# Six wide block products instead of five in the second MLP product of a transformer block on one Trainium2 core

## The chip, the cores and the metric

The kernel runs on one core of one Trainium2 chip. A core has a matrix engine (TensorE, PE in the profile, PEld for its weight loads), a vector engine (VectorE, DVE), a scalar engine (ScalarE, ACT), GpSimd (POOL) and SyncE (SP), which issues most transfers. They work side by side, each through its own queue in order, and wait for each other through semaphores. Matmul results go to eight banks of PSUM (512 float32 values a partition each); VectorE and ScalarE read them from there. The metric is the time of one execution on the device in microseconds.

## What is computed

A block with two parts over x of shape (1, 2048, 512), float32: linear attention with a softmax feature map, and a token-mixing MLP. The change lies in the last product of the second part.

```python
h = x + attention(layernorm(x))
u = gelu(einsum("bsd,sf->bdf", layernorm(h), w1) + b1)   # (B, D, F), F = 1792
y = einsum("bdf,fs->bds", u, w2) + b2                    # (B, D, S), S = 2048
out = h + transpose(y, 0, 2, 1)                          # (B, S, D)
```

## The kernel before, in words

**Split numbers.** Matmuls run on float32 operands cut into a high part and a low part (`whi` and `wlo` for weights, the two halves of an operand `un` or `uf` for the activations). A product of two such numbers takes three terms: high by high, high by low, low by high.

**Tiles and steps of the second product.** S is cut into 16 token tiles of 128, taken in 8 token pairs `sp`; F into 14 tiles, taken in 7 feature pairs `p`; D into two halves of 256. A step is one (sp, p), 56 in all, in the order of `STEPS`: the seven feature pairs of the first token pair, then of the second, and so on. A step is a 2x2 by 2x2 block product, done with seven block multiplications in place of eight; each multiplies one of seven sums of weight blocks (index a) with one of seven sums of activation blocks (index b) and adds into a bank. The table `PROD` names for each multiplication a, b, the bank and, where it is given, the half of the bank.

**Wide and narrow.** A multiplication is done in one of two forms. `wide` (L1106) sends the high weight against both parts of the activations in one matmul of 512 columns, whose two products stand in the two halves of the bank, and the low weight against the high part in one of 256 columns, added into the first half. The halves are summed later. `narrow` (L1110) takes three matmuls of 256 columns that all add into one half; two multiplications that belong to different sums so share a bank. Before, five multiplications of a step are wide and two are narrow; a token pair needs six banks. The last token pair uses another table, `LAST`, in which all seven are narrow, in four banks.

**Order on TensorE.** The order of TensorE, VectorE and ScalarE is written out by hand (`manual_schedule`). The first step of a token pair (p = 0, the opening step) is one multiplication after another (`products`). The steps p = 1 to 4 go by groups of up to two in `steps`: first all 512-column matmuls of both, then for each the 256-column ones and the narrow products. The steps p = 5 and 6 (the closing block) go through `products` together: each multiplication for both steps, so that the banks are finished one after another. Banks are dealt in turn over all eight (`n_bank`), from three pools.

**Evictions.** After the closing block, ScalarE copies one half of bank 0 (`e`, L1162) and the second halves of the last three banks (`low`, L1164), and VectorE adds up the rest in nine operations (L1165 to L1169 and four of L1172) into `ot`. GpSimd adds `ot` and `low` to the output in memory by accumulating transfers.

**Weights.** w2 comes in groups of two steps: SyncE loads `wraw` (L973), VectorE forms the seven sums (L857 to L859, called by `sums_w2`), ScalarE rounds them to `whi` (L992, `hi_w2`), VectorE takes the difference as `wlo` (L1002, `lo_w2`). There are two buffers for `wlo` and three for `whi`, so each waits until TensorE is done with an older group. These calls stand at every second step. In even token pairs (0, 2, 4, 6) one such call falls into the closing block, and `lo_w2` and `hi_w2` stand between the first two and the last two of the L1172 operations, with the sums behind them; in odd pairs the last call falls at p = 5, so `lo_w2` and the sums stand ahead of the evictions.

Of the kernel before, what the change touches and what calls it, by code (L numbers as in the profile page):

```python
# [11 lines left out]
AF = mybir.ActivationFunctionType  # L12
ALU = mybir.AluOpType
# [6 lines left out]
NT = S // P  # L20
KD = D // P
NF = F // P
NP = NF // 2
HD = D // 2
GRP = 2
# [13 lines left out]
def block_kernel(ctx: ExitStack, tc: tile.TileContext, x, xT, wT, phic, wo, w1, b1, w2, b2,  # L39
                 kvmask, ident_in, out):  # L40
    nc = tc.nc
# [487 lines left out]
    def keep(shape, dt, name, i):  # L529
        return keep_pool.tile(shape, dt, name=name, tag=f"keep{i}")  # L530
# [325 lines left out]
    def sums_of(raw):  # L856
        nc.vector.tensor_add(raw[:, 0:2], raw[:, 1].unsqueeze(1).to_broadcast([P, 2, raw.shape[2]]), raw[:, 2:4])  # L857
        nc.vector.tensor_add(raw[:, 5], raw[:, 1], raw[:, 2])
        nc.vector.tensor_add(raw[:, 6], raw[:, 4], raw[:, 5])  # L859
# [106 lines left out]
    def load_w2(g):  # L966
        slot = g % 3 if g < 4 else (3, 1, 2, 0)[g % 4]
        shape = [P, 7, GRP * P]
        if slot == 3:
            RAW[g] = raw3 if g == 4 else hp.tile(shape, F32, name="wraw3", bufs=1)  # L970
        else:
            RAW[g] = hold(shape, F32, "wraw", slot)
        nc.sync.dma_start(RAW[g][:, 1:5], w2[g])  # L973

    def sums_w2():

        g = done["sums"]
        if g == NGR:
            return
        done["sums"] += 1  # L980
        if g not in RAW:
            load_w2(g)
        sums_of(RAW[g])

    def hi_w2():

        g = done["hi"]
        if g == NGR:
            return
        done["hi"] += 1  # L990
        WH[g] = keep([P, 7, GRP * P], F32R, "whi", g % 3)
        nc.scalar.activation(WH[g], RAW[g], AF.Copy)  # L992

    def lo_w2():

        g = done["lo"]
        if g == NGR:
            return
        done["lo"] += 1
        shape = [P, 7, GRP * P]  # L1000
        wl_ = hp.tile(shape, F32R, name="wlo1", bufs=1) if g % 2 else keep(shape, F32R, "wlo", 3)
        nc.vector.tensor_sub(wl_, RAW[g], WH[g])  # L1002
        for i, step in enumerate(STEPS[g * GRP:(g + 1) * GRP]):
            AW[step] = WH[g][:, :, i * P:(i + 1) * P], wl_[:, :, i * P:(i + 1) * P]
# [80 lines left out]
    for p in range(NEAR, NP):  # L1085
# [1 line left out]
    wst.close()  # L1087
    uo = ctx.enter_context(tc.tile_pool(name="uo", bufs=2, reuse_waits="tile"))

    PROD = ((2, 1, 0, None), (5, 5, 1, None), (0, 0, 2, 0), (1, 4, 2, 1), (3, 6, 3, None), (6, 2, 4, None),  # L1090
            (4, 3, 5, None))

    def products(sp, ps, order):
        for a, b, bk, half in order:
            if half is None:
                for low in range(2):
                    for p in ps:
                        wide(sp, p, a, b, bk, low)
            else:
                for p in ps:  # L1100
                    narrow(sp, p, a, b, bk, half)

    def wide(sp, p, a, b, bk, low):
        w, u = AW[sp, p][low][:, a], UB[p, b]
        o, u = (bank[bk][:, 0], u[:, 0]) if low else (bank[bk], u)
        nc.tensor.matmul(o, w, u, start=p == 0 and not low, stop=p == NP - 1, skip_group_check=True)  # L1106

    def narrow(sp, p, a, b, bk, half):
        for i, (x, y) in enumerate(((0, 0), (0, 1), (1, 0))):
            nc.tensor.matmul(bank[bk][:, half], AW[sp, p][x][:, a], UB[p, b][:, y], start=p == 0 and half == 0 and i == 0,  # L1110
                             stop=p == NP - 1 and i == 2, skip_group_check=True)

    def steps(sp, ps, order):
        for p in ps:
            for a, b, bk, half in order:
                if half is None:
                    wide(sp, p, a, b, bk, 0)
        for p in ps:
            for a, b, bk, half in order:
                if half is None:  # L1120
                    wide(sp, p, a, b, bk, 1)
            for a, b, bk, half in order:
                if half is not None:
                    narrow(sp, p, a, b, bk, half)

    def flat(a):
        return a.rearrange("p k d -> p (k d)")
# [3 lines left out]
    for n, (sp, p) in enumerate(STEPS):  # L1131
        t = 2 * sp
        last = t + 2 == NT
        if n % GRP == 0 and p < NP - 1:
            lo_w2()
            hi_w2()
            sums_w2()
        if p == 0:
            bank = []
            for _ in range(6):  # L1140
                pool = (ps_f, ps_q, ps_b, ps_b)[n_bank % 8 // 2]
                bank.append(pool.tile([P, 2, HD], F32, name="py", tag="pu"))
                n_bank += 1
        order = LAST if last else PROD
        run_on = 3 if last else 2
        if p == 0:
            products(sp, [p], order)
            continue
        if p < NP - run_on:
            if n % GRP == 0 or p == 1:  # L1150
                steps(sp, range(p, min(p + GRP - n % GRP, NP - run_on)), order)
            continue
        if p < NP - 1:
            continue
        products(sp, range(NP - run_on, NP), order)
        e = uo.tile([P, 2, HD], F32, name="e")
        u2 = uo.tile([P, HD], F32, name="u2", bufs=1)
        u3 = uo.tile([P, HD], F32, name="u3")
        if not last:
            ot = uo.tile([P, 2, 2, HD], F32, name="ot", bufs=1)  # L1160
            low = uo.tile([P, 3, HD], F32, name="low")
            nc.scalar.activation(e[:, 1], bank[0][:, 0], AF.Copy)  # L1162
            for i in range(3):
                nc.scalar.activation(low[:, i], bank[3 + i][:, 1], AF.Copy)  # L1164
            nc.vector.tensor_add(e[:, 1], bank[0][:, 1], e[:, 1])  # L1165
            nc.vector.tensor_sub(u2, bank[1][:, 0], e[:, 1])
            nc.vector.tensor_add(u2, bank[1][:, 1], u2)
            nc.vector.tensor_sub(u3, u2, bank[2][:, 0])
            nc.vector.scalar_tensor_tensor(e[:, 0], bank[2][:, 1], -1.0, u2, op0=ALU.mult, op1=ALU.subtract)  # L1169

            def out_block(i, h, o, add):
                nc.vector.scalar_tensor_tensor(ot[:, i, h], o, b2s[:, t + i:t + i + 1], add, op0=ALU.add, op1=ALU.add)  # L1172

            out_block(0, 0, bank[2][:, 1], u3)
            out_block(0, 1, bank[3][:, 0], u3)
            nc.gpsimd.dma_start(out[t * P:(t + 1) * P, :], flat(ot[:, 0]), accum_op=ALU.add)  # L1176
            if n % GRP == 0:
                lo_w2()
                hi_w2()
            out_block(1, 0, bank[4][:, 0], e[:, 0])  # L1180
            out_block(1, 1, bank[5][:, 0], e[:, 1])
            nc.gpsimd.dma_start(out[(t + 1) * P:(t + 2) * P, :], flat(ot[:, 1]), accum_op=ALU.add)
            nc.gpsimd.dma_start(out[t * P:(t + 1) * P, HD:D], low[:, 0], accum_op=ALU.add)
            nc.gpsimd.dma_start(out[(t + 1) * P:(t + 2) * P, :], flat(low[:, 1:3]), accum_op=ALU.add)
            if n % GRP == 0:
                sums_w2()
            continue

        hb = [uo.tile([P, 2, HD], F32, name=f"hb{i}", bufs=1) for i in range(2)]
        for i in range(2):  # L1190
            nc.sync.dma_start(flat(hb[i]), out[(t + i) * P:(t + i + 1) * P, :])
            nc.vector.tensor_scalar(hb[i], hb[i], b2s[:, t + i:t + i + 1], None, op0=ALU.add)
        nc.scalar.activation(e[:, 1], bank[0][:, 0], AF.Copy)
        nc.vector.tensor_add(hb[1][:, 1], bank[0][:, 0], hb[1][:, 1])
        nc.vector.tensor_sub(u2, bank[0][:, 1], e[:, 1])
        nc.vector.tensor_sub(hb[1][:, 0], hb[1][:, 0], u2)
        nc.vector.tensor_sub(u3, u2, bank[1][:, 0])
        nc.vector.tensor_add(hb[0], hb[0], u3.unsqueeze(1).to_broadcast([P, 2, HD]))
        nc.vector.tensor_add(hb[0][:, 0], bank[1][:, 1], hb[0][:, 0])
        nc.vector.tensor_sub(hb[1][:, 0], hb[1][:, 0], bank[1][:, 1])  # L1200
        nc.vector.tensor_add(hb[0][:, 1], bank[2][:, 0], hb[0][:, 1])
        nc.sync.dma_start(out[t * P:(t + 1) * P, :], flat(hb[0]))
        for k, o, q in ((0, bank[2][:, 1], nc.scalar), (1, bank[3][:, 0], nc.sync)):
            nc.vector.tensor_add(hb[1][:, k], o, hb[1][:, k])
            q.dma_start(out[(t + 1) * P:NT * P, k * HD:(k + 1) * HD], hb[1][:, k])
# [49 lines left out]
```

## Time and profile before

| | |
|---|---|
| median of 3 runs | 518.52 us (518.47 to 518.72) |
| the profiled execution, its own time | 518.56 us |
| its span, first to last instruction | 516.8 us |
| granted TensorE clock | 1.00 |
| first row of the second product (`py`), and the last (start) | 354.0 us, 513.3 us |
| length of a token pair from the second to the seventh | 17.24 and 17.26 us in turn |

A row of the timeline gives the start, the duration and, for several instructions in one row, their count; the engine, the line, the operation, its output and inputs and the shape. In brackets stands how long the engine was idle before it and what released it. A row of busy time by stretch gives, for each engine, the busy time and the number of instructions that started there, then TensorE's granted clock, the DMA share and the rate. Durations of matmuls overlap, so their cost is read from the distance of their starts.

### The profile page before, as it was taken

To read this page: it belongs to the slowest core of one execution; us is meant where nothing else is said; L and a number is where in the kernel's file an instruction comes from. 1 tells how busy PE (TensorE), PEld (TensorE's weight loads), DVE (VectorE), ACT (ScalarE), POOL (GpSimd) and SP (SyncE) were. 2 spreads that over 40 slices of the span, in tenths; PEclk is the share of its full clock that TensorE was granted. 3 is DMA by queue.
4 is the path that set the end of the run, shared out by engine and by line. 5 is a ranking of instruction groups with operands and counts; after the bars stand their busy time and mean duration, and the time that the engine had idled before them with its cause. 6 is when DMAs were issued, how large, how long until landed. Compare 5 with 4: busy or idle time off the path is not lost.

```text
span 516.8 us, 9476 instructions
## 1 busy us (share of the span) xinstructions
PE 510.9 (99%) x3595; PEld 442.9 (86%) x3595; DVE 445.5 (86%) x789; ACT 296.8 (57%) x494; POOL 245.0 (47%) x188
## 2 busy tenths in 40 slices
PE   9999999999999999999999999999999999999997
PEld 8888888887877778777788899998889999899997
DVE  6893999986799998777796998989989898988985
ACT  6998944434255876668976643457653434434430
POOL 2479799975999999985343200000002212212220
PEclk9999999999999999999999999999999999999999
DMA  8744310000041324334322233374135787677843
GB/s 313 270 127 122 81 53 29 1 1 3 12 154 41 103 84 140 124 124 122 115 89 83 82 105 104 99 245 141 43 123 117 162 192 171 119 162 159 191 50 77
DMA packets 36300, 58.56 MB, mean 113 GB/s; under 512 B 3744, under 2 KB 19360, under 8 KB 36256
## 3 DMA queue, kind: packets, MB, share of 16 engines
q1 hardware_dynamic: 31648, 50.85, 31.3%
q0 software_dynamic: 4032, 6.42, 9.9%
q8 instruction: 28, 0.46, 0.4%
q10 hardware_dynamic: 576, 0.69, 0.4%
q14 instruction: 16, 0.13, 0.1%
HBM read 46.81 MB, written 11.14 MB: 112 GB/s over the span
## 4 chain that ended last, share of the span: by engine, by line
PE 89%; POOL 7%; DVE 2%; ACT 1%; issue 1%; POOLq 0%
PE py L1106 17%; PE pu L936 12%; PE py L1110 10%; PE pu L66 7%; PE pu L67 7%; PE pu L68 7%; PE pv L67 3%; PE pv L68 3%; PE pv L66 3%; PE pk_ps L66 2%; PE pk_ps L68 2%; PE pk_ps L67 2%; POOL ez L456 2%; POOL eq L474 2%; PE po L68 2%; PE tn L548 2%
## 5 line engine op out<-in xcount | busy, mean ns | idle before, releaser
L1176 POOL DMA_DIRECT2D out<-ot x7 | 6.2, 884 | 142.1 <-DVE ot L1172 142.1
L992 ACT ACTIVATE whi<-wraw 128x1792 fp32r<-128x1792 f32 x28 | 47.6, 1701 | 44.1 <-DVE wraw L859 20.3
L1002 DVE TENSOR_TENSOR wlo<-wraw,whi 128x1792 fp32r<-128x1792 f32 x28 | 56.6, 2021 | 8.4 <-PE py L1110 6.9
L67 PE MATMUL pu<-hs,whi 128*128 128x512 f32 x128 | 50.3, 393 | 1.2 <-POOL hs L62 1.2
L66 PE MATMUL pu<-hs,whi 128*128 128x512 f32 x128 | 50.1, 399 | 0.0
L1106 PE MATMUL py<-uf,whi 128*128 128x512 f32 x175 | 48.4, 393 | 0.0
L68 PE MATMUL pu<-hs,wlo 128*128 128x512 f32 x128 | 48.0, 390 | 0.0
L897 ACT ACTIVATE whi<-wraw 128x896 fp32r<-128x896 f32 x24 | 22.9, 954 | 31.2 <-PE pu L936 26.4
L456 POOL TENSOR_TENSOR ez<-eq,zB 128x1024 f32<-128x1024 f32 x16 | 38.3, 2399 | 4.4 <-ACT zB L503 4.4
L1110 PE MATMUL py<-uf,whi 128*128 128x256 f32 x210 | 39.0, 283 | 0.0
L936 PE MATMUL pu<-ht,whi 128*128 128x256 f32 x192 | 35.6, 283 | 0.0
L208 POOL TENSOR_TENSOR pk<-pk,sk 128x1024 f32<-128x1024 f32 x16 | 30.9, 1938 | 7.3 <-DVE sk L207 7.2
L62 POOL TENSOR_TENSOR hs<-hb,hs 128x512 fp32r<-128x512 f32 x16 | 22.4, 1400 | 23.9 <-ACT hs L61 23.8
L550 ACT ACTIVATE pht<-tn 128x512 f32<-128x512 f32 x32 | 17.4, 595 | 28.4 <-PE tn L548 28.3
L474 POOL TENSOR_TENSOR eq<-eq,w 128x1024 f32<-128x1024 f32 x16 | 32.4, 2028 | 1.3 <-DVE w L471 1.2
L1110 PEld LDWEIGHTS py<-uf,whi 128*128 128x128 f32 x210 | 32.7, 192 | 0.0
L1106 PEld LDWEIGHTS py<-uf,whi 128*128 128x128 f32 x175 | 29.8, 189 | 3.5
L212 POOL TENSOR_TENSOR zacc<-zacc,pk 128x1024 f32<-128x1024 f32 x13 | 31.2, 2399 | 0.5
L1106 PEld LDWEIGHTS py<-uf,wlo 128*128 128x128 f32 x175 | 27.9, 190 | 4.0
L66 PEld LDWEIGHTS pu<-hs,whi 128*128 128x128 f32 x128 | 24.1, 188 | 7.2 <-issue 2.5
L936 PEld LDWEIGHTS pu<-ht,whi 128*128 128x128 f32 x192 | 30.0, 192 | 0.0
L1110 PE MATMUL py<-uf,wlo 128*128 128x256 f32 x105 | 29.7, 283 | 0.0
(207 smaller groups left out, 1625.0 us busy)
## 6 DMA issues: line engine op xcount, KB each, us to landing
wraw<-in_w SPq DMA_DIRECT2D x28, 512.0 KB, 4.5
wraw<-in_w SPq DMA_DIRECT2D x48, 256.0 KB, 2.8
xraw<-in_xT SPq DMA_DIRECT2D x16, 256.0 KB, 3.1
xh<-in_x SPq DMA_DIRECT2D x16, 256.0 KB, 2.7
h<-in_x SPq DMA_DIRECT2D x16, 256.0 KB, 2.7
out<-h SPq DMA_DIRECT2D x14, 256.0 KB, 2.7
out<-ot POOLq DMA_DIRECT2D x14, 256.0 KB, 4.8
wraw<-in_wT SPq DMA_DIRECT2D x12, 256.0 KB, 4.6
```

The lines of the kernel that those rows point to most:

```text
L66: nc.tensor.matmul(o, ah, bh, start=first, stop=False)
L67: nc.tensor.matmul(o, ah, bl, start=False, stop=False)
L68: nc.tensor.matmul(o, al, bh, start=False, stop=last)
L208: nc.gpsimd.tensor_mul(heads(PK[t]), heads(PK[t]), sk.unsqueeze(2).to_broadcast([P, 2 * H, DH]))
L212: nc.gpsimd.tensor_add(zacc, zacc, PK[t])
L456: nc.gpsimd.tensor_mul(EZ[t], EQ[t], zB)
L474: nc.gpsimd.tensor_mul(heads(EQ[t]), heads(EQ[t]), W[t].rearrange("p g c h -> p (g c h)").unsqueeze(2).to_broadcast([P, 2 * H, DH]))
L936: nc.tensor.matmul(ACC[p][bk][:, half], WS[p, i][x][:, a], hb[b][y], start=i == 0 and half == 0 and k == 0, stop=i == NT // 2 - 1 and k == ...
L992: nc.scalar.activation(WH[g], RAW[g], AF.Copy)
L1002: nc.vector.tensor_sub(wl_, RAW[g], WH[g])
L1106: nc.tensor.matmul(o, w, u, start=p == 0 and not low, stop=p == NP - 1, skip_group_check=True)
L1110: nc.tensor.matmul(bank[bk][:, half], AW[sp, p][x][:, a], UB[p, b][:, y], start=p == 0 and half == 0 and i == 0, stop=p == NP - 1 and i == ...
```

## The change

The multiplication (0, 0), which was narrow in half 0 of bank 2, becomes wide in bank 2; (1, 4) stays narrow and moves to half 0 of a bank of its own; the rest move up by one. A token pair has seven banks, the last pair four (it was dealt six and used four). VectorE gets one more subtraction, of the second half of bank 2. The two `lo_w2`/`hi_w2` calls move behind the last eviction, but not in the pair before the last (`ahead`); in odd pairs the sums that stood at p = 5 move behind the evictions. In the first token pair the seventh multiplication is held back to the second step, and done there for both.

```diff
-    PROD = ((2, 1, 0, None), (5, 5, 1, None), (0, 0, 2, 0), (1, 4, 2, 1), (3, 6, 3, None), (6, 2, 4, None),
-            (4, 3, 5, None))
+    PROD = ((2, 1, 0, None), (5, 5, 1, None), (0, 0, 2, None), (1, 4, 3, 0), (3, 6, 4, None), (6, 2, 5, None),
+            (4, 3, 6, None))
...
         if n % GRP == 0 and p < NP - 1:
             lo_w2()
             hi_w2()
-            sums_w2()
+            if p < NP - 2 or last:
+                sums_w2()
         if p == 0:
             bank = []
-            for _ in range(6):
+            for _ in range(4 if last else 7):
...
         if p == 0:
-            products(sp, [p], order)
+            products(sp, [p], order[:-1] if n == 0 else order)
+            continue
+        if n == 1:
+            steps(sp, [p], order[:-1])
+            products(sp, [0, p], order[-1:])
             continue
...
-                nc.scalar.activation(low[:, i], bank[3 + i][:, 1], AF.Copy)
+                nc.scalar.activation(low[:, i], bank[4 + i][:, 1], AF.Copy)
...
             nc.vector.tensor_sub(u3, u2, bank[2][:, 0])
-            nc.vector.scalar_tensor_tensor(e[:, 0], bank[2][:, 1], -1.0, u2, op0=ALU.mult, op1=ALU.subtract)
+            nc.vector.tensor_sub(u3, u3, bank[2][:, 1])
+            nc.vector.scalar_tensor_tensor(e[:, 0], bank[3][:, 0], -1.0, u2, op0=ALU.mult, op1=ALU.subtract)
...
-            if n % GRP == 0:
+            ahead = t + 4 == NT
+            if ahead:
                 lo_w2()
                 hi_w2()
-            out_block(1, 0, bank[4][:, 0], e[:, 0])
-            out_block(1, 1, bank[5][:, 0], e[:, 1])
+            out_block(1, 0, bank[5][:, 0], e[:, 0])
+            out_block(1, 1, bank[6][:, 0], e[:, 1])
+            if n % GRP == 0 and not ahead:
+                lo_w2()
+                hi_w2()
...
-            if n % GRP == 0:
-                sums_w2()
+            sums_w2()
```

TensorE in the closing block of the first token pair, third and fourth multiplication, for both steps (`py` and its number is a bank, `uf` an operand of the activations). Before:

```order
L1110 MATMUL py_4488<-uf_4433,whi_4479 128x256 x2
L1110 MATMUL py_4488<-uf_4433,wlo_4524 128x256
L1110 MATMUL py_4488<-uf_4459,whi_4526 128x256 x2
L1110 MATMUL py_4488<-uf_4459,wlo1_4564 128x256
L1110 MATMUL py_4488<-uf_4446,whi_4479 128x256 x2
L1110 MATMUL py_4488<-uf_4446,wlo_4524 128x256
L1110 MATMUL py_4488<-uf_4465,whi_4526 128x256 x2
L1110 MATMUL py_4488<-uf_4465,wlo1_4564 128x256
```

and now:

```order
L1106 MATMUL py_4488<-uf_4433,whi_4479 128x512
L1106 MATMUL py_4488<-uf_4459,whi_4525 128x512
L1106 MATMUL py_4488<-uf_4433,wlo_4523 128x256
L1106 MATMUL py_4488<-uf_4459,wlo1_4561 128x256
L1110 MATMUL py_4489<-uf_4446,whi_4479 128x256 x2
L1110 MATMUL py_4489<-uf_4446,wlo_4523 128x256
L1110 MATMUL py_4489<-uf_4465,whi_4525 128x256 x2
L1110 MATMUL py_4489<-uf_4465,wlo1_4561 128x256
```

Twelve matmuls became ten, and they fill two banks instead of one.

TensorE in the opening step of the second token pair, from its second multiplication on (in brackets what a row waits for). Before:

```order
L1106 MATMUL py_4653<-un0_3275,whi_4526 128x512
L1106 MATMUL py_4653<-un0_3275,wlo1_4564 128x256
L1110 MATMUL py_4654<-un0_3275,whi_4526 128x256 [waits DVE_49]
L1110 MATMUL py_4654<-un0_3275,whi_4526 128x256
L1110 MATMUL py_4654<-un0_3275,wlo1_4564 128x256
L1110 MATMUL py_4654<-un0_3275,whi_4526 128x256 x2
L1110 MATMUL py_4654<-un0_3275,wlo1_4564 128x256
L1106 MATMUL py_4655<-un0_3275,whi_4526 128x512 [waits DVE_49,PE_49]
L1106 MATMUL py_4655<-un0_3275,wlo1_4564 128x256
L1106 MATMUL py_4656<-un0_3275,whi_4526 128x512 [waits DVE_49]
```

and now:

```order
L1106 MATMUL py_4648<-un0_3275,whi_4525 128x512 [waits DVE_49]
L1106 MATMUL py_4648<-un0_3275,wlo1_4561 128x256
L1106 MATMUL py_4649<-un0_3275,whi_4525 128x512 [waits DVE_49,PE_49]
L1106 MATMUL py_4649<-un0_3275,wlo1_4561 128x256
L1110 MATMUL py_4650<-un0_3275,whi_4525 128x256 [waits DVE_49,PE_49]
L1110 MATMUL py_4650<-un0_3275,whi_4525 128x256
L1110 MATMUL py_4650<-un0_3275,wlo1_4561 128x256
L1106 MATMUL py_4651<-un0_3275,whi_4525 128x512 [waits DVE_49]
L1106 MATMUL py_4651<-un0_3275,wlo1_4561 128x256
L1106 MATMUL py_4652<-un0_3275,whi_4525 128x512 [waits DVE_49]
```

The second bank already waits for VectorE, where the third did; two multiplications wait for two semaphores, where one did.

VectorE at the end of the second token pair, an odd one. Before:

```order
L857 TENSOR_TENSOR wraw_4760<-wraw_4760 128x512
L858 TENSOR_TENSOR wraw_4760<-wraw_4760 128x256
L859 TENSOR_TENSOR wraw_4760<-wraw_4760 128x256
L1165 TENSOR_TENSOR e_4797<-py_4652,e_4797 128x256
L1166 TENSOR_TENSOR u2_4798<-py_4653,e_4797 128x256
L1167 TENSOR_TENSOR u2_4798<-py_4653,u2_4798 128x256
L1168 TENSOR_TENSOR u3_4799<-u2_4798,py_4654 128x256
L1169 SCALAR_TENSOR_TENSOR e_4797<-py_4654,u2_4798 128x256
L1172 SCALAR_TENSOR_TENSOR ot_4800<-py_4654,b2s_65,u3_4799 128x256
L1172 SCALAR_TENSOR_TENSOR ot_4800<-py_4655,b2s_65,u3_4799 128x256
L1172 SCALAR_TENSOR_TENSOR ot_4800<-py_4656,b2s_65,e_4797 128x256
L1172 SCALAR_TENSOR_TENSOR ot_4800<-py_4657,b2s_65,e_4797 128x256
```

and now:

```order
L1002 TENSOR_TENSOR wlo1_4747<-wraw_4673,whi_4710 128x1792
L1170 TENSOR_TENSOR e_4781<-py_4647,e_4781 128x256
L1171 TENSOR_TENSOR u2_4782<-py_4648,e_4781 128x256
L1172 TENSOR_TENSOR u2_4782<-py_4648,u2_4782 128x256
L1173 TENSOR_TENSOR u3_4783<-u2_4782,py_4649 128x256
L1174 TENSOR_TENSOR u3_4783<-u3_4783,py_4649 128x256
L1175 SCALAR_TENSOR_TENSOR e_4781<-py_4650,u2_4782 128x256
L1178 SCALAR_TENSOR_TENSOR ot_4784<-py_4650,b2s_65,u3_4783 128x256
L1178 SCALAR_TENSOR_TENSOR ot_4784<-py_4651,b2s_65,u3_4783 128x256
L1178 SCALAR_TENSOR_TENSOR ot_4784<-py_4652,b2s_65,e_4781 128x256
L1178 SCALAR_TENSOR_TENSOR ot_4784<-py_4653,b2s_65,e_4781 128x256
L857 TENSOR_TENSOR wraw_4804<-wraw_4804 128x512
```

The sums moved from ahead of the evictions to behind them, and ten operations stand in a row.

More of the change, by code (lines that the diff above doesn't have):

```diff
@@ L1168, in block_kernel @@
             nc.vector.tensor_sub(u3, u2, bank[2][:, 0])
-            nc.vector.scalar_tensor_tensor(e[:, 0], bank[2][:, 1], -1.0, u2, op0=ALU.mult, op1=ALU.subtract)
+            nc.vector.tensor_sub(u3, u3, bank[2][:, 1])
+            nc.vector.scalar_tensor_tensor(e[:, 0], bank[3][:, 0], -1.0, u2, op0=ALU.mult, op1=ALU.subtract)
             def out_block(i, h, o, add):
                 nc.vector.scalar_tensor_tensor(ot[:, i, h], o, b2s[:, t + i:t + i + 1], add, op0=ALU.add, op1=ALU.add)
-            out_block(0, 0, bank[2][:, 1], u3)
-            out_block(0, 1, bank[3][:, 0], u3)
+            out_block(0, 0, bank[3][:, 0], u3)
+            out_block(0, 1, bank[4][:, 0], u3)
             nc.gpsimd.dma_start(out[t * P:(t + 1) * P, :], flat(ot[:, 0]), accum_op=ALU.add)
-            if n % GRP == 0:
+            ahead = t + 4 == NT
+            if ahead:
                 lo_w2()
                 hi_w2()
-            out_block(1, 0, bank[4][:, 0], e[:, 0])
-            out_block(1, 1, bank[5][:, 0], e[:, 1])
+            out_block(1, 0, bank[5][:, 0], e[:, 0])
[3 more added lines that the diff above has]
+                hi_w2()
             nc.gpsimd.dma_start(out[(t + 1) * P:(t + 2) * P, :], flat(ot[:, 1]), accum_op=ALU.add)
```

## The prediction, made before the changed kernel ran

> **What bounds the kernel now.** I read the page's first part, then the busy time by stretch, and then the timelines of TensorE, VectorE and ScalarE in two token pairs of the second MLP product.
>
> ```profile
> PE 510.9 (99%) x3595; PEld 442.9 (86%) x3595; DVE 445.5 (86%) x789; ACT 296.8 (57%) x494; POOL 245.0 (47%) x188
> core 0: us, PE busy (x) PEld busy (x) DVE busy (x) ACT busy (x) POOL busy (x), PEclk, DMA share, GB/s
> 390.35:407.59 17.24, 17.24 (x114) 15.74 (x113) 15.31 (x21) 8.12 (x8) 3.65 (x4) 1.00 0.68 142
> 407.59:424.85 17.26, 17.26 (x114) 15.74 (x113) 15.79 (x26) 6.54 (x7) 3.46 (x4) 1.00 0.80 172
> 513.60:516.80 3.20, 0.00 (x0) 0.00 (x0) 0.42 (x1) 0.00 (x0) 0.00 (x0) 1.00 0.45 164
> ```
>
> TensorE is busy through both pairs, 17.25 us each, at a granted clock of 1.00. VectorE is busy for 15.3 to 15.8 us of that, so it is the next limit and not a far one. Behind the last matmul lies a tail of 3.2 us that the change does not enter. The time can move only by what TensorE has to issue, or by a wait that comes up on it. Its price list stands in its own timeline, of an odd pair's last four steps and the next pair's first:
>
> ```profile
> 399.67 2.46 PE L1106 MATMUL py<-uf,whi 128*128 128x512 f32 x10
> 401.96 0.76 PE L1106 MATMUL py<-uf,wlo 128*128 128x256 f32 x5
> 402.56 0.40 PE L1110 MATMUL py<-uf,whi 128*128 128x256 f32 x2
> ...
> 402.92 0.40 PE L1110 MATMUL py<-uf,whi 128*128 128x256 f32 x2
> ...
> 404.60 0.63 PE L1106 MATMUL py<-uf,whi 128*128 128x512 f32 x2
> ...
> 405.99 0.40 PE L1110 MATMUL py<-uf,whi 128*128 128x256 f32 x2
> ...
> 409.52 0.40 PE L1106 MATMUL py<-un,whi 128*128 128x512 f32 x1
> ...
> 411.99 0.86 PE L1106 MATMUL py<-un,whi 128*128 128x512 f32 x3
> ```
>
> The start times give the spacing (durations overlap). Ten matmuls of 512 columns: 401.96 - 399.67 = 2.29, so 0.229 us each. Five of 256: 0.60, so 0.120. A narrow product, three of 256: 402.92 - 402.56 = 0.36. A wide one, a 512 and a 256: 0.349. In the closing block of a pair, where two steps alternate, four wide products (two of each step) take 405.99 - 404.60 = 1.39, 0.3475 each.
>
> **What is removed.** In each of 7 x 7 = 49 steps (the last pair keeps its order) one narrow product becomes wide: 16 matmuls become 15 and the columns stay 768. That saves 0.36 - 0.349 = 0.011 in the four steps of the inner form and 0.0125 in the three of the closing and opening form: per pair 4 x 0.011 + 3 x 0.0125 = 0.08, in seven pairs 0.57. Against it stands that a wait for two semaphores now sits at two products of an opening step instead of one. The opening step above lasts 411.99 - 409.52 = 2.47 where its five wide and two narrow products would make 5 x 0.3475 + 0.72 = 2.46; so such a wait costs 0.01 at most, 0.07 over seven pairs. The bounds are 0.47 and 0.61 (all 49 at 0.0125). I take 0.55, since most products keep their form.
>
> The Trainium skill speaks for less: "TensorE: Matmul & The Clock Gate", section "Back-to-back issue gap", gives a matmul of N columns N/2.4 + 2.5 ns, so only 2.5 ns for each one dropped, an estimated 0.12 us for 49 of them. By that page 256 columns take 109 ns and 512 take 216; the rows show 120 and 229, so this trace does not bear it out, and the measured spacing decides.
>
> **What is added on VectorE.** One 128x256 subtraction from a bank per pair. Below are VectorE's rows at the end of the odd pair above (its closing block starts at F = 404.60) and ScalarE's.
>
> ```profile
> 404.87 2.03 DVE L1002 TENSOR_TENSOR wlo<-wraw,whi 128x1792 fp32r<-128x1792 f32 x1 [1.26 <-PE py L1110]
> 406.81 0.68 DVE L857 TENSOR_TENSOR wraw<-wraw 128x512 f32<-128x512 f32 x1
> ...
> 408.33 0.42 DVE L1165 TENSOR_TENSOR e<-py,e 128x256 f32<-128x256 f32 x1
> 408.86 0.42 DVE L1166 TENSOR_TENSOR u<-py,e 128x256 f32<-128x256 f32 x1
> 409.31 0.42 DVE L1167 TENSOR_TENSOR u<-py,u 128x256 f32<-128x256 f32 x1
> 409.84 0.42 DVE L1168 TENSOR_TENSOR u<-u,py 128x256 f32<-128x256 f32 x1
> 410.18 0.42 DVE L1169 SCALAR_TENSOR_TENSOR e<-py,u 128x256 f32<-128x256 f32 x1
> 410.52 0.87 DVE L1172 SCALAR_TENSOR_TENSOR ot<-py,b2s,u 128x256 f32<-128x256 f32 x2
> 411.30 0.87 DVE L1172 SCALAR_TENSOR_TENSOR ot<-py,b2s,e 128x256 f32<-128x256 f32 x2
> 412.08 2.02 DVE L1002 TENSOR_TENSOR wlo<-wraw,whi 128x1792 fp32r<-128x1792 f32 x1
> 404.73 1.71 ACT L992 ACTIVATE whi<-wraw 128x1792 fp32r<-128x1792 f32 x1 [2.70 <-PE py L1110]
> 406.34 0.36 ACT L1162 ACTIVATE e<-py 128x256 f32<-128x256 f32 x1
> ```
>
> The nine evictions take 412.08 - 408.33 = 3.75. The tenth needs its forerunner's result, as L1167 needs L1166's, which started 0.45 later: 0.46 us, so 4.21. And the even pair:
>
> ```profile
> 419.65 2.03 DVE L1002 TENSOR_TENSOR wlo<-wraw,whi 128x1792 fp32r<-128x1792 f32 x1 [0.58 <-PE py L1110]
> 423.17 0.42 DVE L1165 TENSOR_TENSOR e<-py,e 128x256 f32<-128x256 f32 x1
> ...
> 424.89 0.42 DVE L1168 TENSOR_TENSOR u<-u,py 128x256 f32<-128x256 f32 x1 [0.31 <-PE py L1110]
> 425.56 0.92 DVE L1172 SCALAR_TENSOR_TENSOR ot<-py,b2s,u 128x256 f32<-128x256 f32 x2
> 426.87 2.03 DVE L1002 TENSOR_TENSOR wlo<-wraw,whi 128x1792 fp32r<-128x1792 f32 x1 [0.38 <-PE py L1106]
> 428.81 0.87 DVE L1172 SCALAR_TENSOR_TENSOR ot<-py,b2s,e 128x256 f32<-128x256 f32 x2
> 422.75 0.39 ACT L1162 ACTIVATE e<-py 128x256 f32<-128x256 f32 x1 [1.53 <-PE py L1106]
> 426.98 0.39 ACT L1164 ACTIVATE low<-py 128x256 f32<-128x256 f32 x1 [0.31 <-PE py L1106]
> ```
>
> In these two pairs VectorE waits for TensorE for 1.26 + 0.58 + 0.31 + 0.38 = 2.53 us. Two added operations take 0.92 of it, so VectorE keeps some 1.6 us and the addition costs nothing, as long as nothing that TensorE needs comes late. Without that cover it would cost 0.46 a pair, 3.2 in all.
>
> **Whether TensorE waits for a bank.** This is the part that could cost. Seven banks a pair leave one spare, so the opening step of the next pair writes its second to seventh bank into the old first to sixth. The closing block is now six wide and one narrow double product, 6 x 0.695 + 0.72 = 4.89, so the old banks are wanted at F + 5.24, 5.58, 5.93, 6.29, 6.64 and 6.98.
>
> In an odd pair the sums of raw weights (406.81 to 408.33, 1.52 us) now follow the evictions. VectorE is then free at F + 2.21, and ScalarE's copy, which is behind its own whi, ends at 406.70, F + 2.10: in time. The ten operations start at F + 2.21, 2.74, 3.19, 3.72, 4.18, 4.52, 4.86, 5.25, 5.64 and 6.03. Their last reads of the six banks end at F + 2.63, 3.61, 4.60, 5.34, 5.73 and 6.12. The margins are 2.6, 2.0, 1.3, 0.95, 0.91 and 0.86 us: thin, but no wait. Left where they were, the sums would put all of it 1.52 later and TensorE would stand for about 0.66.
>
> In an even pair (F = 421.86, one pair of 17.26 later) the first eviction starts at F + 1.31, bound by the copy (422.75 to 423.14); the margin at the old sixth bank is above 1.6. The wait of 0.31 for the two narrow products goes, since the third bank is complete after one wide product instead of two narrow ones (F + 2.09 instead of 2.83), and it is first read at F + 2.83. The last output waits for ScalarE's third low copy (F + 5.51) and VectorE is free at F + 5.94.
>
> **What is queued behind the evictions.** The low weights (L1002) that stood inside them in even pairs start at F + 5.94 instead of 426.87 = F + 5.01 and end at F + 7.97. TensorE wants them after the opening step (2.45) and twelve matmuls of 512 columns (2.75), at F + 10.1: 2.1 to spare. In odd pairs the sums come at F + 6.42, the low weights at 7.94 to 9.97, wanted after two steps and twelve matmuls at F + 12.5. The raw weights' loads on SyncE wait for L1002's, which move by under 1 us; no L857 row above shows VectorE waiting for a load. GpSimd's transfers of ot start with the evictions, earlier in odd pairs, and nothing on TensorE waits for them. In the pair before the last the low weights stay in their old place, so the last pair, which is all narrow, keeps its supply.
>
> **The first pair** holds back its seventh bank, which a gelu (L800) still reads:
>
> ```profile
> 377.26 1.37 ACT L800 ACTIVATE u<-pu,b1s 128x512 f32<-128x512 f32 x2 [4.72 <-PE pu L68]
> 377.74 1.07 PE L1106 MATMUL py<-un,whi 128*128 128x512 f32 x4
> ```
>
> Both gelus end at 378.63. TensorE's product there comes after two 512 columns, five 256 and a narrow product, 1.42 after the last pu matmul, near 379.2: 0.5 to spare, at no cost. The sum: 518.56 - 0.55 = 518.01; the profiled execution is 0.04 above the median of the runs, so 518.0.
>
> **The rivals.** (A) The forecast: only TensorE's issue shrinks, 518.0.
>
> (B) Slower: the evictions of odd pairs come too late for the next opening step. Speaking for it: the smallest margin, 0.86 us, rests on VectorE finishing its low weights at F + 2.21 and on ten starts in a row without a slip, on an engine that is busy for nine tenths. Against: each start comes from a row in which the same operations run. If they came as late as they do now (408.33, F + 3.73), three odd pairs would cost 0.66 each: 518.0 + 2.0 = 520.0. The price begins at a delay of 0.86; the kernel is slower than before from a delay of 0.86 + 0.55/3 = 1.04 us.
>
> (C) The change has no price: what a matmul costs beyond its columns hides behind weight loads, and 768 columns stay 768: 518.5. Against it the 0.229 and 0.120 of neighbouring rows. The skill's gap above is this case nearly, at 518.4.
>
> (D) Weight loads pace TensorE (86% busy), and time goes by their number: 17.25 / 112 = 0.154 a load, 49 fewer are 7.5 us, 511.0. Against it: a 512 takes nearly twice a 256, though each has one load.
>
> **How the numbers follow.** A 0.70, B 0.14, C 0.10, D 0.06. A difference of 0.2%, 1.04 us, is about what a measurement of this kernel can tell from no change. A and C lie within it; of B a small part does, and of D too, if a part of the loads counts. Faster 0.06, same 0.78, slower 0.16. The predicted time is A's. A's own spread is 517.9 to 518.1; the range goes up through C and the first part of B to 518.9 and down to 517.5, which leaves out most of B and D, under 2 in 10.
>
> **What would show it.** L1106 with 588 matmuls (490 now) and L1110 with 294 (441 now); a pair in 17.17; the first eviction of odd pairs near F + 2.2; VectorE's waits for TensorE near 1.6 per two pairs; the tail at 3.2. Gaps on TensorE at a pair's opening step, released by VectorE, would mean B; pairs of 17.25 C; of 16.2 D. A new wait of TensorE for L1002, or for a load, would be a case that I have priced at nothing.

## The result, and the profile after

The changed kernel takes 517.66 us, the median of 15 runs (517.07 to 518.23), against 518.46 for the kernel before on the same chip (15 runs, 518.03 to 519.19): a ratio of 0.9985, 95% interval 0.9978 to 0.9992. That is 0.80 us or 0.15% faster: inside the 0.2% that the prediction took as the least that can be told from no change, though the interval leaves out 1. The profiled execution has a span of 515.8 us (before: 516.8).

The page's busy time of the changed kernel, then its busy time by stretch for an odd pair, an even pair and the tail:

```profile
PE 509.8 (99%) x3546; PEld 439.6 (85%) x3546; DVE 448.3 (87%) x796; ACT 297.1 (58%) x494; POOL 244.9 (47%) x188
```

```profile
387.08:404.23 17.15, 17.15 (x108) 15.36 (x107) 15.74 (x26) 6.54 (x7) 3.66 (x4) 1.00 0.69 147
404.23:421.37 17.14, 17.14 (x108) 15.34 (x107) 16.37 (x24) 8.24 (x8) 3.46 (x4) 1.00 0.74 167
512.65:515.80 3.15, 0.00 (x0) 0.00 (x0) 0.42 (x1) 0.00 (x0) 0.00 (x0) 1.00 0.46 167
```

Matmuls fell from 3595 to 3546, by 49, one for each step that was changed; VectorE got seven operations more. TensorE is still busy through the whole pair at a clock of 1.00. The same view over five whole pairs, from the opening row of the second pair to that of the seventh, of the kernel before:

```profile
392.28:478.52 86.24, 86.24 (x562) 78.71 (x561) 77.75 (x113) 37.44 (x38) 17.53 (x20) 1.00 0.74 157
```

and of the changed one:

```profile
391.97:477.69 85.72, 85.72 (x528) 76.77 (x526) 79.45 (x119) 37.70 (x38) 17.49 (x20) 1.00 0.75 164
```

The five pairs are 86.24 - 85.72 = 0.52 us shorter, 0.104 each, and TensorE is busy through all of them. The change takes 35 matmuls out of these pairs and adds five subtractions on VectorE; the rows differ by 34 and 6, since the new order also moves a few operations across the edges of the stretch.

For the experiments I read the length of the whole second product from the chain of waits (start, duration, engine, what it works on, line, count): from the end of the last block of the first product (L936, 504 matmuls) to the end of the last block of matmuls. Before:

```profile
292.80 60.47 PE pu L936 x504
...
495.94 17.64 PE py L1110 x147
```

and after:

```profile
292.69 60.47 PE pu L936 x504
...
494.99 17.64 PE py L1110 x147
```

Before, this is (495.94 + 17.64) - (292.80 + 60.47) = 160.31 us, after 159.47: 0.84 less. Where the second product begins differs by another 0.11, ahead of anything that the change touches; together 0.95 of the 1.0 between the two spans, which are rounded to 0.1. The tail of 3.2 us is the same to that rounding. Medians of the same kernel wander by up to 0.36 us from one set of runs to the next, while this length repeated to the hundredth (below), so it decides between theories.

TensorE's timeline after: the opening row of the second pair, then of the third pair the opening step with that step's narrow product and the wide one behind it, the second step, the closing block and the next opening:

```profile
391.97 0.40 PE L1106 MATMUL py<-un,whi 128*128 128x512 f32 x1
...
409.12 0.40 PE L1106 MATMUL py<-un,whi 128*128 128x512 f32 x1
...
410.16 0.40 PE L1110 MATMUL py<-un,whi 128*128 128x256 f32 x2
...
410.51 0.40 PE L1106 MATMUL py<-un,whi 128*128 128x512 f32 x1
...
411.56 1.55 PE L1106 MATMUL py<-un,whi 128*128 128x512 f32 x6
...
421.37 0.63 PE L1106 MATMUL py<-uf,whi 128*128 128x512 f32 x2
...
426.25 0.40 PE L1106 MATMUL py<-un,whi 128*128 128x512 f32 x1
```

and the opening rows, the second step and the closing block before:

```profile
392.28 0.40 PE L1106 MATMUL py<-un,whi 128*128 128x512 f32 x1
...
409.52 0.40 PE L1106 MATMUL py<-un,whi 128*128 128x512 f32 x1
...
411.99 1.32 PE L1106 MATMUL py<-un,whi 128*128 128x512 f32 x5
...
421.86 0.63 PE L1106 MATMUL py<-uf,whi 128*128 128x512 f32 x2
...
426.78 0.40 PE L1106 MATMUL py<-un,whi 128*128 128x512 f32 x1
```

In the third pair (sp = 2, an even one) the opening step went from 2.47 to 2.44, the four inner steps from 9.87 to 9.81, the closing block from 4.92 to 4.88 (each to 0.01 or so). That pair went from 17.26 to 17.13, the second pair, an odd one, from 17.24 to 17.15. VectorE's timeline after, end of the odd pair whose closing block starts at F = 404.23:

```profile
404.50 2.02 DVE L1002 TENSOR_TENSOR wlo<-wraw,whi 128x1792 fp32r<-128x1792 f32 x1 [1.06 <-PE py L1110]
406.44 0.42 DVE L1170 TENSOR_TENSOR e<-py,e 128x256 f32<-128x256 f32 x1
...
409.86 0.87 DVE L1178 SCALAR_TENSOR_TENSOR ot<-py,b2s,e 128x256 f32<-128x256 f32 x2
410.64 0.68 DVE L857 TENSOR_TENSOR wraw<-wraw 128x512 f32<-128x512 f32 x1
...
422.68 0.43 DVE L1170 TENSOR_TENSOR e<-py,e 128x256 f32<-128x256 f32 x1
...
426.87 0.49 DVE L1178 SCALAR_TENSOR_TENSOR ot<-py,b2s,e 128x256 f32<-128x256 f32 x1 [0.21 <-ACT low L1169]
427.27 2.02 DVE L1002 TENSOR_TENSOR wlo<-wraw,whi 128x1792 fp32r<-128x1792 f32 x1
```

The ten evictions of the odd pair start at F + 2.21 and leave VectorE free at F + 6.41. In the even pair (F = 421.37) they start at F + 1.31, the last output waits for ScalarE's copy until F + 5.50, and the low weights follow at F + 5.90.

### The profile page after: what moved, and what is told of

The parts are those of the page before. It is cut to its first block, busy times and chain, and to the rows that moved or that the text cites. A ratio compares the mean times of both kernels' runs of the same rounds, so it can differ in the third digit from the quotient of the medians.

```text
span 515.8 us, 9392 instructions
## 1 busy us (share of the span) xinstructions
PE 509.8 (99%) x3546; PEld 439.6 (85%) x3546; DVE 448.3 (87%) x796; ACT 297.1 (58%) x494; POOL 244.9 (47%) x188
## 3 DMA queue, kind: packets, MB, share of 16 engines
q0 software_dynamic: 4032, 6.42, 9.9%
## 4 chain that ended last, share of the span: by engine, by line
PE 87%; POOL 7%; DVE 2%; ACT 2%; issue 1%; DMA 1%; SPq 0%; POOLq 0%; ACTq 0%
PE py L1106 20%; PE pu L936 12%; PE pu L66 7%; PE pu L67 7%; PE pu L68 7%; PE py L1110 7%; PE pv L67 3%; PE pv L68 3%; PE pv L66 3%; PE pk_ps L66 3%; PE pk_ps L67 2%; PE pk_ps L68 2%; POOL ez L456 2%; POOL eq L474 2%; PE po L68 2%; PE tn L548 2%
## 5 line engine op out<-in xcount | busy, mean ns | idle before, releaser
L992 ACT ACTIVATE whi<-wraw 128x1792 fp32r<-128x1792 f32 x28 | 47.7, 1702 | 44.2 <-DVE wraw L859 26.6
L1002 DVE TENSOR_TENSOR wlo<-wraw,whi 128x1792 fp32r<-128x1792 f32 x28 | 56.6, 2020 | 4.9 <-PE py L1110 4.7
L1106 PE MATMUL py<-uf,whi 128*128 128x512 f32 x210 | 57.6, 394 | 0.0
L1106 PEld LDWEIGHTS py<-uf,whi 128*128 128x128 f32 x210 | 35.8, 189 | 4.3
L1106 PEld LDWEIGHTS py<-uf,wlo 128*128 128x128 f32 x210 | 33.1, 190 | 4.6
L936 PE MATMUL pu<-ht,whi 128*128 128x256 f32 x192 | 35.6, 283 | 0.0
L1106 PE MATMUL py<-uf,wlo 128*128 128x256 f32 x210 | 34.9, 281 | 0.0
L66 PEld LDWEIGHTS pu<-hs,whi 128*128 128x128 f32 x128 | 24.1, 188 | 7.1 <-issue 2.5
L936 PEld LDWEIGHTS pu<-ht,whi 128*128 128x128 f32 x192 | 30.0, 192 | 0.0
L67 PEld LDWEIGHTS pu<-hs,whi 128*128 128x128 f32 x128 | 24.1, 188 | 6.6 <-POOL hs L62 2.1
L68 PEld LDWEIGHTS pu<-hs,wlo 128*128 128x128 f32 x128 | 23.9, 188 | 4.8
```

What stands on the lines that cost most here:

```text
L66: nc.tensor.matmul(o, ah, bh, start=first, stop=False)
L67: nc.tensor.matmul(o, ah, bl, start=False, stop=False)
L68: nc.tensor.matmul(o, al, bh, start=False, stop=last)
L936: nc.tensor.matmul(ACC[p][bk][:, half], WS[p, i][x][:, a], hb[b][y], start=i == 0 and half == 0 and k == 0, stop=i == NT // 2 - 1 and k == ...
```

## The experiments

All against the kernel before on the same chip. "Second product" is the length just defined. The ratio is the one on record; it is not quite the quotient of the two medians. "Sums first" has 5 runs, "low weights early" 6, the first row 15 and the others 11.

| kernel | median us | before, same runs | ratio, 95% interval | second product us |
|---|---|---|---|---|
| changed | 517.66 | 518.46 | 0.9985 (0.9978 to 0.9992) | 159.47 |
| changed, again | 517.72 | 518.51 | 0.9989 (0.9980 to 0.9998) | 159.47 |
| changed, a third time | 517.37 | 518.15 | 0.9986 (0.9977 to 0.9995) | 159.47 |
| only the order moved | 518.14 | 518.22 | 1.0000 (0.9991 to 1.0009) | 160.31 |
| seven banks, still narrow | 518.11 | 518.22 | 0.9998 (0.9990 to 1.0007) | 160.28 |
| narrow over two halves | 518.49 | 518.15 | 1.0006 (0.9997 to 1.0015) | 160.28 |
| three wide ones split | 519.24 | 518.22 | 1.0022 (1.0013 to 1.0031) | 161.22 |
| sums first | 519.98 | 518.51 | 1.0036 (1.0023 to 1.0048) | 161.92 |
| low weights in between | 519.48 | 518.51 | 1.0019 (1.0010 to 1.0027) | 161.11 |
| seven wide | 517.31 | 518.22 | 0.9982 (0.9973 to 0.9991) | 159.31 |
| seven wide, again | 517.44 | 518.51 | 0.9978 (0.9969 to 0.9987) | 159.67 |
| seven wide, low weights early | 516.64 | 518.15 | 0.9969 (0.9958 to 0.9981) | 158.93 |

**Which part gains: the moved order alone.** The kernel before with its six banks, and only VectorE's order as in the change.

```diff
-            sums_w2()
+            if p < NP - 2 or last:
+                sums_w2()
...
-            if n % GRP == 0:
+            ahead = t + 4 == NT
+            if ahead:
                 lo_w2()
                 hi_w2()
...
+            if n % GRP == 0 and not ahead:
+                lo_w2()
+                hi_w2()
...
-            if n % GRP == 0:
-                sums_w2()
+            sums_w2()
```

> The kernel before, with its six banks and two narrow products, and only the moved order on VectorE (low weights and sums behind the evictions). Theory (the gain is TensorE's issue alone, the order only protects it): no change, 518.4 to 518.6, a token pair stays at 17.25 us. Rival (the order on VectorE brings the gain): 517.7, a pair near 17.15.

Its chain:

```profile
292.30 60.47 PE pu L936 x504
...
495.44 17.64 PE py L1110 x147
```

513.08 - 352.77 = 160.31, to the hundredth that of before. The order gains nothing by itself. (The kernel before stood at 518.22 in this set of runs, 0.24 below the first set, so the absolute times that were expected of this set's kernels are some 0.2 high.)

**Seven banks without the wide form.** The changed kernel, with (0, 0) narrow again in its own bank; the added subtraction goes, as there is no second half.

```diff
-    PROD = (... (0, 0, 2, None), (1, 4, 3, 0), ...
+    PROD = (... (0, 0, 2, 0), (1, 4, 3, 0), ...
...
-            nc.vector.tensor_sub(u3, u3, bank[2][:, 1])
```

> The changed kernel with (0, 0) narrow again, but alone in the first half of bank 2; seven banks and the order as changed, the second subtraction left out. Theory: 16 matmuls a step as before, so 518.3 to 518.6 and a pair near 17.25. Rival (two narrow products in one bank cost more than their matmuls, or the banks' order brings part of the gain): between 517.7 and 518.3, a pair below 17.22.

```profile
292.63 60.47 PE pu L936 x504
...
495.74 17.64 PE py L1110 x147
```

160.28: the gain is gone but for 0.03. The fewer matmuls carry it, not the banks. The 0.03 lies ahead of the second pair's opening; every pair from the second on takes 17.24 or 17.26 as before.

**More matmuls at the same columns.** The changed kernel, with three of its six wide 512-column matmuls of each step sent as two of 256 into the same two halves: 3 x 49 = 147 matmuls more, columns, banks and evictions unchanged.

```diff
+        if not low and a in (4, 5, 6) and sp < NT // 2 - 1:
+            for k in range(2):
+                nc.tensor.matmul(bank[bk][:, k], w, u[:, k], start=p == 0 and k == 0, stop=p == NP - 1,
+                                 skip_group_check=True)
+            return
```

> The changed kernel, but three of the six wide products send the high weight in two matmuls of 256 columns to the two halves instead of one of 512: 18 matmuls a step at the same columns, banks and evictions. Theory: 3 x 49 matmuls more at 0.011 to 0.017 us, 1.6 to 2.5 us above the changed kernel, 519.3 to 520.1, a pair near 17.4 to 17.5. Rival (a matmul more at the same columns is free): 517.7. Rival (weight loads pace TensorE at 0.15 us each): over 20 us more.

```profile
292.93 60.47 PE pu L936 x504
...
496.97 17.65 PE py L1115 x147
```

161.22, so 1.75 us for 147 matmuls: 0.0119 each. A matmul more, which here comes with one more weight load (3693 loads for 3546), has a price at equal columns, and it is close to the 0.011 to 0.0125 that neighbouring rows gave.

**What the moved order protects: the sums.** In the changed kernel the sums of raw weights go back ahead of an odd pair's evictions.

```diff
-            if p < NP - 2 or last:
-                sums_w2()
+            sums_w2()
...
-            sums_w2()
+            if n % GRP == 0:
+                sums_w2()
```

> The changed kernel with the sums of odd pairs back ahead of the evictions. Theory (the spare of 0.86 us at the old sixth bank is what keeps TensorE going): the evictions start 1.52 later, TensorE stands about 0.66 us at the opening step behind each of three odd pairs, released by VectorE; 2.0 us above the changed kernel, 519.4 to 519.8. Rival (the moved order protects nothing, since TensorE has enough slack elsewhere): 517.4 to 517.7, no gap on TensorE.

The view of TensorE's waits in the second product (waited for: us in total, times, longest), which is empty for the changed kernel, and VectorE's and TensorE's timelines of this one (its evictions stand one line higher in the file, L1169 for L1170):

```profile
PE py L1110 <- DVE u L1173: 0.5, 3, 0.2
```

```profile
408.32 0.42 DVE L1169 TENSOR_TENSOR e<-py,e 128x256 f32<-128x256 f32 x1
```

```profile
409.47 0.40 PE L1106 MATMUL py<-un,whi 128*128 128x512 f32 x1
...
410.85 0.48 PE L1110 MATMUL py<-un,whi 128*128 128x256 f32 x2 [0.17 <-DVE u L1173]
...
411.48 0.50 PE L1106 MATMUL py<-un,whi 128*128 128x512 f32 x1
...
412.72 0.63 PE L1106 MATMUL py<-un,whi 128*128 128x512 f32 x2
```

The first eviction starts at 408.32, at F + 3.74 if that closing block, as in the changed kernel, began 4.89 before the opening row (409.47), in place of F + 2.21, and the opening step's narrow product waits for the bank that L1173 still reads. That happens three times, once for each odd pair whose successor uses the wide table. The second product takes 161.92, 2.45 more than the changed kernel's or 0.82 for each odd pair. In the opening step shown the narrow product stands 410.85 - 409.47 = 1.38 behind the step's start, in the changed kernel 410.16 - 409.12 = 1.04: 0.34 late. The whole step takes 412.72 - 409.47 = 3.25 in place of 2.44, so another 0.47 came behind that start: the next wide product starts 411.48 - 410.85 = 0.63 behind the narrow one in place of 0.35, and the three wide ones take 1.24 in place of 1.05. The idle time that the wait rows name, 0.5 over three pairs, is only a part of that, so this view can be small, or empty, where TensorE has lost time; the distances of starts tell more. The median, 2.26 above the changed kernel's in the same runs, is a little above what was expected.

**What the moved order protects: the low weights.** In the changed kernel all even pairs do `lo_w2` and `hi_w2` between the outputs again.

```diff
-            ahead = t + 4 == NT
+            ahead = n % GRP == 0
```

> The changed kernel with the low and high weights of even pairs back between the outputs, in all four even pairs instead of the last one only. Theory: the old sixth bank is read until F + 7.42 instead of F + 5.33, wanted at F + 6.98, so TensorE stands about 0.5 us at the opening step behind each of three even pairs (the fourth is as before): 1.4 to 1.6 us above the changed kernel, 518.9 to 519.2. Rival (no cost, as the spare bank covers it): 517.4 to 517.7.

```profile
PE py L1106 <- DVE ot L1178: 0.9, 3, 0.3
```

```profile
427.21 2.03 DVE L1002 TENSOR_TENSOR wlo<-wraw,whi 128x1792 fp32r<-128x1792 f32 x1
429.15 0.87 DVE L1178 SCALAR_TENSOR_TENSOR ot<-py,b2s,e 128x256 f32<-128x256 f32 x2
```

The last two outputs come behind 2 us of low weights, and a wide product of the next opening step waits for the bank they read. 161.11: 1.64 more than the changed kernel, 0.55 for each of three even pairs, a little above the 0.5 expected; the median of 519.48 lies above its range too. With seven banks a pair either old order loses more than the change gains.

**The last narrow product too.** All seven wide: the matmuls fall by another 49. ScalarE copies the second half of the new wide bank, and VectorE does one operation more.

```diff
-    PROD = (... (1, 4, 3, 0), ...
+    PROD = (... (1, 4, 3, None), ...
...
+            nc.scalar.activation(e[:, 0], bank[3][:, 1], AF.Copy)
...
-            nc.vector.scalar_tensor_tensor(e[:, 0], bank[3][:, 0], -1.0, u2, op0=ALU.mult, op1=ALU.subtract)
+            nc.vector.tensor_add(e[:, 0], bank[3][:, 0], e[:, 0])
...
-            out_block(0, 0, bank[3][:, 0], u3)
+            out_block(0, 0, e[:, 0], u3)
+            nc.vector.scalar_tensor_tensor(e[:, 0], e[:, 0], -1.0, u2, op0=ALU.mult, op1=ALU.subtract)
```

> The changed kernel with (1, 4) wide as well: 14 matmuls a step instead of 15, one more subtraction and one more copy at each eviction. Theory: every matmul less at the same 768 columns saves TensorE 0.011 to 0.017 us, so 0.55 to 0.8 us below the changed kernel, 516.9 to 517.1, and a pair near 17.05; the old fifth and sixth bank are read 0.46 and 0.42 us ahead of their next use, so no wait. Rival (VectorE becomes the limit, the chain of eleven comes too late): TensorE gaps at the opening steps of the next pair, 0.1 us or more each, and no gain, 517.7 or more.

```profile
494.67 2.02 DVE wlo L1002
496.74 15.15 PE py L1110 x124
```

The chain now passes through VectorE: the last pair waits for its low weights, which come behind a longer row of evictions. The second product takes 159.31, only 0.16 less than the changed kernel's. Theory and rival each held in part: the pairs became shorter as expected, 17.06 and 17.07 us, but some 0.38 was lost, at the last pair and not at the opening steps of the others.

**The changed kernel and the seven-wide one again,** unaltered, in another set of runs:

> The changed kernel as it stands, again, beside the seven wide products on the same chip: 0.7 to 0.8 us below the kernel before. Rival (the first measurement was high by its noise, and the gain is that of my sum): 0.55 below.

> All seven products wide, again, beside the changed kernel. Theory: a pair is shorter by 17.145 - 17.06 = 0.085 us, seven of them 0.6 us below the changed kernel, 1.3 to 1.4 below the kernel before. Rival (something gives it back outside the pairs): 0.1 to 0.2 us below the changed kernel.

The changed kernel repeats at 159.47. The seven-wide one takes 159.67 this time, and its timeline shows why; VectorE reaches the sums before the load of raw weights has landed:

```profile
436.59 0.69 DVE L857 TENSOR_TENSOR wraw<-wraw 128x512 f32<-128x512 f32 x1 [0.27 <-DMA wraw<-in_w]
```

The way from there to TensorE leads through ScalarE, which the same trace shows. Its rounding (L992) waits for these sums and starts at 438.37, its copy of bank 0 behind it at 439.98; in the fastest version (below), whose pairs stand 0.06 earlier here, these are at 437.95 and 439.56. VectorE's first eviction then waits for that copy:

```profile
440.38 0.42 DVE L1171 TENSOR_TENSOR e<-py,e 128x256 f32<-128x256 f32 x1 [0.24 <-ACT e L1167]
```

The pair that opens behind it takes 17.41 us in place of 17.07: a transfer 0.27 late has reached TensorE. TensorE's wait view is empty all the same. So neither the 0.6 below the changed kernel that was expected nor the rival's 0.1 to 0.2 came; it was 0.28.

**Seven wide, low weights ahead of all outputs.** The same, with the block that the pair before the last does early moved from behind the second output to ahead of the first.

```diff
+            ahead = t + 4 == NT
+            if ahead:
+                lo_w2()
+                hi_w2()
             out_block(0, 0, e[:, 0], u3)
...
-            ahead = t + 4 == NT
-            if ahead:
-                lo_w2()
-                hi_w2()
```

> Seven wide products, with the low weights of the pair before the last moved ahead of that pair's outputs, since they came 0.27 us late there for the all-narrow last pair. Theory: that wait goes, the second product (from the last L936 matmul's block to the last matmul) takes 158.9 to 159.0 us instead of 159.31 with seven wide and 159.47 in the changed kernel; 0.4 to 0.6 us below the changed kernel. Rival (VectorE has no spare left, and the loss comes back at another place): 159.3, no difference from seven wide before.

```profile
292.23 60.47 PE pu L936 x504
...
493.99 17.64 PE py L1110 x147
```

158.93: the last pair's 0.38 are back. This is the fastest version, 516.64 us, 0.9969 (0.9958 to 0.9981) of before. VectorE's waits for TensorE ahead of L1002 are 0.9 us over three pairs, where the changed kernel has 3.2. Its opening rows of the second, third and fourth pair:

```profile
391.45 0.40 PE L1106 MATMUL py<-un,whi 128*128 128x512 f32 x1
...
408.51 0.40 PE L1106 MATMUL py<-un,whi 128*128 128x512 f32 x1
...
425.58 0.40 PE L1106 MATMUL py<-un,whi 128*128 128x512 f32 x1
```

The odd pair takes 17.06, the even one 17.07.

**Is it the bank's half?** A narrow product sends three matmuls into one half. Here (0, 0) is narrow, but its middle matmul goes into the other half, and the evictions stay as in the change.

```diff
-    PROD = (... (0, 0, 2, None), (1, 4, 3, 0), ...
+    PROD = (... (0, 0, 2, 0), (1, 4, 3, 0), ...
...
-            nc.tensor.matmul(bank[bk][:, half], AW[sp, p][x][:, a], UB[p, b][:, y], ...
+            to = 1 if i == 1 and bk == 2 and sp < NT // 2 - 1 else half
+            nc.tensor.matmul(bank[bk][:, to], AW[sp, p][x][:, a], UB[p, b][:, y], ...
```

> The changed kernel with (0, 0) as three matmuls of 256 columns in a row, at the place of the narrow product, but into the two halves as the wide one fills them; the evictions are those of the changed kernel. It tells what a narrow product costs above its matmul count. Theory 1 (three 256-column matmuls in a row with three weight loads slow their neighbours): as with the narrow product alone in its bank, 160.2 to 160.3 us for the second product. Theory 2 (adding twice into the same half costs the surplus): 160.0 to 160.1. Rival (the price lies in the evictions): 159.5.

```profile
292.46 60.47 PE pu L936 x504
...
495.57 17.64 PE py L1111 x147
```

160.28, as with one half, though it has the change's evictions on VectorE. So 0.81 of the 0.84 lies in how TensorE is given the work, and none of it in which half the sums go to or in who reads them. That three weight loads in a row slow their neighbours, as the first theory has it, is not shown by this; its time came true, its mechanism was not tried.

**The changed kernel a third time,** with those two:

> The changed kernel, a third time, beside the two above on the same chip: 159.47 us for the second product, 0.6 to 0.8 us below the kernel before.

Again 159.47.

## Why the prediction was right, and which term was off

**The bound held.** TensorE's wait view of the second product is empty before and after, the changed kernel's pairs from the second to the seventh all take 17.13 to 17.15 us, and the time moved by what TensorE has to issue. The moved order alone gave nothing, the seven banks without the wide form gave 0.03, and 147 matmuls more at equal columns cost 1.75. Forecast A was 518.0 and the measured time is 517.66, inside its range; 0.84 us came off the second product where 0.55 were predicted.

**The mis-sized term** is the price of the narrow product: "0.011 in the four steps of the inner form and 0.0125 in the three of the closing and opening form", less up to 0.07 for a second wait on two semaphores. The price was read from rows of an odd pair and taken for all seven pairs. There it was nearly right: the second pair gave 17.24 - 17.15 = 0.09 where 0.08 were predicted. An even pair gave 0.12 to 0.13 (17.26 to 17.13 in the rows shown): 0.06 in the inner steps (0.044 predicted), 0.04 in the closing block (0.025), 0.03 in the opening step (0.0125, less the second wait). So the second wait had no price that can be seen. The part up to the second pair's opening row, the first pair with its products between those of the first MLP product, is 39.01 before (392.28 - 353.27) and 38.81 after (391.97 - 353.16): 0.20 where 0.08 were predicted, of which 0.03 came with the seven banks and the multiplication held back. Five regular pairs make 0.52 and the seventh 0.12, which sums to the 0.84; the last pair takes the same in both.

**The evictions** came where the sums of starts had put them: F + 2.21 and free at F + 6.41 (predicted 2.21 and 6.42) in the odd pair, F + 1.31, 5.50 and 5.90 (1.31, 5.51, 5.94) in the even one. VectorE's waits for TensorE were put at 1.6 per two pairs; 1.06 were left, ahead of L1002, and 0.2 behind ScalarE's copy.

**Rival B** is a real mechanism that the new order keeps out. Sums left ahead were priced at 0.66 a pair and cost 0.82, 0.34 of it ahead of the first product that waits and the rest behind its start.

**Rival C** falls with the split matmuls: 0.0119 us for each, where C has nothing. The Trainium skill's gap of 2.5 ns ("TensorE: Matmul & The Clock Gate", "Back-to-back issue gap"), which that section gives for a matmul by itself, would make 147 of them an estimated 0.37 us; the measured 1.75 does not bear it out for this stream of weight loads and matmuls.

**Rival D** falls with the same run: 147 more weight loads at its 0.154 would have cost over 22 us.

**What stays open.** After the change, the second narrow product's removal (seven wide, low weights early) gave 0.54 us over the 49 steps, 0.011 each, and the split matmuls cost 0.0119. The first one's removal gave 0.84, or 0.017 each on average. It is tempting to put the difference down to the two narrow products standing in a row, but the pairs speak against that as the whole reason. In an odd pair the two removals gave the same, 17.24 to 17.15 to 17.06, 0.013 a step each, though there too the two had stood in a row. In an even pair they gave 17.26 to 17.13 to 17.07, and in the first pair 0.20 and 0.06. Odd pairs take their inner steps in two groups of two, even pairs as one, two and one, and in the first pair they stand between other work; so the cost goes with the place. That the neighbours on TensorE set it is likely, but no run tries it.

## What to carry to other kernels

On a TensorE that never waits, count matmuls as well as columns: merging two matmuls into one paid 0.011 to 0.017 us here, and its price can be read beforehand from the starts of neighbouring rows, best from every kind of place in which it occurs: one odd pair's rows forecast that pair to 0.01 and the whole only to two thirds. Such a merge takes banks, and then the deadline of each old bank has to be set against the start of each eviction; here the order of work on VectorE gained nothing, yet with either half of the old order the changed kernel's second product was 1.6 or 2.5 us longer. When the next such step takes the rest of the other engine's spare time, look for the work that its longest row pushes back: one block moved ahead of the outputs was worth 0.38 us.

## What the runs showed of the hardware

A 256-column matmul more with its weight load, at equal columns, cost 11.9 ns with nothing else altered (147 of them, 1.75 us). A narrow product has one matmul more than a wide one and cost 17 ns more on average where two stood in each step, whichever half of the bank it fed, and 11 ns where it was the only one; by place, the first of these was 13 ns in odd pairs and 17 in even ones, the second 13 and 9. The changed kernel repeated the length of its second product to 0.01 us in three profiles, while medians of one kernel moved by 0.36 between sets of runs (518.51 and 518.15 before): a change of a tenth of a percent is better read from a stage of the trace than from times.
